# All w_out copies of the weights stored on ScalarE's queue

## The chip, the cores and the metric

The kernel runs on one core of a Trainium2 chip. The metric is the device time of one execution in microseconds (us). PE is TensorE, DVE is VectorE, ACT is ScalarE, POOL is GpSimd and SP is SyncE, which here does nothing but send transfers; ACT sends transfers too, between its own instructions, from one and the same instruction stream.

## The reference, cut to what matters

```python
# q, k, v: 8 x 8 x 576 x 64; a causal window of 64 keys
scores = scale * np.matmul(q, k.transpose(0, 1, 3, 2))
scores = np.where((rel >= 0) & (rel < 64), scores, -1e9)
attn = softmax(scores)
x = (attn @ v).transpose(0, 2, 1, 3).reshape(4608, 512)
h = x @ w_in                       # w_in 512 x 2048, w_out 2048 x 512
g = np.maximum(0.01 * h, h)
out = g @ w_out
```

The weights come as 64-bit floats. The kernel brings them to single precision itself, and splits each single into a high and a low part, so that every product is three products of the parts.

## The kernel before, in words

**The weights.** There are 32 pieces of 128x512 numbers, numbered n: even n is block n/2 of w_in, odd n is block n//2 of w_out. Piece n passes eight small steps, all named with n in a list written by hand (ORDER): `raw` sends the load of the 64-bit words (512 KB, on ACT's queue but for the first three, buffer `raw`, three of them), `bits`, `sign`, `clamp` and `join` on DVE and `abs` on ACT make the single-precision copy `w` (pool tag "o", two buffers), `chi` (function `split`) takes the high part on ACT and also stores `w` to the DRAM tensor `w_single` (256 KB), `rest` takes the low part on DVE. A buffer of `w` is free for a later `join` when the piece in it has had its `rest` and its store has landed. The stored copies are read again much later (`prepare`), to make sums of weight blocks.

**The first stage.** Until about 165 us of the span, PE works through ORDER: attention on pairs of query blocks m (two halves b = 2m, 2m+1: scores `S`, mask and shield `E`, column maximum `P` on POOL, its subtraction `N` or `sub`, `exp`, product with the values `V`, the sums and the quotient `sm`, `rec`, `y` on DVE, transposition `T`, parts of x `H` on ACT and `L` on DVE), and the feed-forward products `M` (h = x w_in) and `W` (g w_out), with `lk`, `gh` on ACT and `gl` on DVE between them. Loads of q, k, v for pair m are sent by SP (`q`, `k`, `v`). In ORDER each engine's instructions stand in the order in which the code issues them, and no engine passes over an instruction that waits.

**The later stages.** A planner (`arrange`) sets the order for the remaining attention and for products that save multiplications (lines 1196 and 1262); all of their inputs come from the first stage.

**Transfer semaphores.** Each transfer that SP or ACT sends takes the next of eight semaphores (DMAHW0 to DMAHW7), over both queues together. Before it is sent, the engine waits until the last transfer that took this semaphore has landed, unless it has already waited for that. In the order below a wait on DMAHW3 is such a wait, or a wait for data.

Of the kernel before, what the change touches and what calls it, by code (L numbers as in the profile page):

```python
# [105 lines left out]
def flat(t):  # L106
    return t.rearrange("p a b -> p (a b)") if len(t.shape) == 3 else t
# [3 lines left out]
def band_attention_ffn(ctx: ExitStack, tc: tile.TileContext, qk, vW, vL, w_in, w_out, eye_mask, out, outT):  # L111
    nc = tc.nc
# [88 lines left out]
    w_single = dram.tile([2, FT, P, 512], F32, name="w_single")  # L201
# [7 lines left out]
    raws, singles = {}, {}  # L209
# [8 lines left out]
    def parts(n):  # L218
        while n // 2 >= len(wi):
            late_weights(len(wi))  # L220
        return (wi, wo)[n % 2][n // 2]
# [27 lines left out]

    def split(n):  # L250
        nc.scalar.copy(flat(parts(n)[0]), singles[n])
        (nc.sync if n % 2 else nc.scalar).dma_start(w_single[n % 2, n // 2], singles[n])

    def rest(n):
        hi, lo = (flat(x) for x in parts(n))
# [200 lines left out]
    def mm2(c, f, part):  # L456


        gh, gl = g.pop((c, f, part.start))
        wh, wl = wo[f]  # L460
        for i in range(part.start // P, part.stop // P):
            split = c == 1 or c == 0 and i < 2
            begin = f == 0 or split and f == half
            end = f == FT - 1 or split and f == half - 1
            if begin:
                pool, tag = (ps_o, f"o{i}")
                if c == 1 and f == 0 and i > 1:
                    pool, tag = ps_e, "st"[i - 2]
                acc[c, i] = pool.tile([P, DM], F32, tag=tag, name=f"acc{c}_{i}_{f}")
            ts = slice(i * P, (i + 1) * P)  # L470
            for n, (a, b) in enumerate(((gh, wh), (gh, wl), (gl, wh))):
                nc.tensor.matmul(
                    acc[c, i], a[:, ts], b, start=begin and n == 0, stop=end and n == 2
                )
            if end:
                due.append(partial(evict, c, i, f, split))

    def evict(c, i, f, split):
        ps = acc.pop((c, i))
        o = probs_of[:, i % 2]  # L480
        nc.scalar.copy(o, ps)
        sums[c, i] = dram.tile([P, DM], F32, name=f"sum{c}_{i}")
        nc.sync.dma_start(sums[c, i], o)
# [26 lines left out]
    def begin(k):  # L510
        steps[k] = mm1(*jobs[k])

    acts = dict(
        S=scores, E=shield, Z=lambda b: add_mask(0, banks[b], False), P=top, N=take, sub=minus, exp=exps, V=values_q, sm=total, rec=inverse, y=product, T=turn, H=high_x, L=low_x,
        raw=fetch_w, bits=bits, sign=sign, abs=size, clamp=clamp, join=join, chi=split, rest=rest, q=load_q, k=load_k, v=load_v,
        X=idle, M=begin, lk=lambda k: steps[k][0](), gh=lambda k: steps[k][1](), gl=lambda k: steps[k][2](), W=lambda k: mm2(*jobs[k]),
        ev=lambda k: due.pop(0)(),
# [188 lines left out]
    for name in late.split():  # L706
        kind = name.rstrip("0123456789")
        n = int(name[len(kind) :])
# [473 lines left out]
    def filled(of, *after):  # L1182
        n = next(fills)
        return n, op("POOL", 0.6, partial(fill, n, of), *tile_free[n % RING], *after, rank=0.2, land=7.0)
# [236 lines left out]
    for s in range(NS):  # L1421
        for f in range(half):
# [4 lines left out]
            for k in range(7):  # L1427
                p, b = 7 * f + k, bank_at(s, BANK[k])
                if p % 4 == 0:
                    made_before = [] if s else [y for x in range(f, min(f + 2, half)) for y in prepared[0, x]]  # L1430
                    n, got = filled(w_first[:, 512 * p : 512 * (p + 4)], *made_before)
# [97 lines left out]
```

## Time and profile before

| what | value |
|---|---|
| median of 3 runs | 859.99 us (859.66, 859.99, 2631.46) |
| the profiled execution | 859.84 us, of which the span is 858.1 us |
| PE busy in the span | 838.6 us (98%) |
| DVE, ACT, POOL busy | 638.9, 376.4, 382.4 us |
| mean granted clock of PE | 0.992 |

The profiled execution is 0.15 us under the median, and 1.7 us of it lie outside the span. A matmul of 128x512 takes 0.39 us by the profile's rows but is followed by the next after 0.23 us, since they overlap; an engine's idle time is what stands in square brackets in a timeline, with what ended it.

### The profile page before, as it was taken

Reading aid. Unit: us, or ns where it says so; the run is one execution under the profiler, and the core shown is the slowest. Engines: PE = TensorE matmul, PEld = TensorE weight load, DVE = VectorE, ACT = ScalarE, POOL = GpSimd, SP = SyncE. Lnnn points to the kernel's source line nnn. Section 1 sums busy time; section 2 is a strip of 40 time slices with the busy share of each in tenths; the row PEclk is TensorE's granted clock in tenths of the full one; section 3 lists DMA queues with packets and bytes.
Section 4 is the critical chain, followed back from the end, with each engine's and each line's share of the span. In section 5 each row is a group of like instructions: output and inputs, shape, how many; then the busy total and the mean of one; then the engine's idle time right before and its main releaser. Section 6 shows DMA issues by size and latency. Waiting matters only on the chain.

```text
span 858.1 us, 16755 instructions
## 1 busy us (share of the span) xinstructions
PE 838.6 (98%) x6736; PEld 682.0 (79%) x6736; DVE 638.9 (74%) x912; ACT 376.4 (44%) x599; POOL 382.4 (45%) x216
## 2 busy tenths in 40 slices
PE   7899999899999999999999999999999999999998
PEld 4777888788788888788788888888888888888886
DVE  5888886576768789798759988676589874546864
ACT  4565654433433435454535443343354433334431
POOL 4322000288788762685876114878863111111110
PEclk9899999999999999999999999999999999999999
DMA  7778578879898979999999898879988997677682
GB/s 270 234 236 268 167 222 297 289 262 327 299 310 308 337 247 296 332 355 375 355 260 316 245 279 268 257 228 298 283 236 240 265 284 202 195 192 192 183 221 96
DMA packets 130861, 225.75 MB, mean 263 GB/s; under 512 B 15840, under 2 KB 53600, under 8 KB 130784
## 3 DMA queue, kind: packets, MB, share of 16 engines
q0 software_dynamic: 53568, 88.09, 37.5%
q10 hardware_dynamic: 34304, 74.16, 26.6%
q1 hardware_dynamic: 42912, 62.43, 21.9%
q8 instruction: 53, 0.87, 0.4%
q14 instruction: 24, 0.20, 0.1%
HBM read 167.28 MB, written 57.26 MB: 262 GB/s over the span
## 4 chain that ended last, share of the span: by engine, by line
PE 51%; DMA 2%; DVE 1%; issue 0%; ACT 0%; ACTq 0%; DVEq 0%
PE z L1262 27%; PE m L1196 22%; PE o L811 2%; DMA p<-w_single 1%; PE s L283 1%; DMA rows<-late_c 1%; DVE pspare L1111 0%; DVE p L1205 0%; DVE pxa L1205 0%; DVE qk L1282 0%; DVE p L1105 0%; ACT p L1108 0%; DVE e L759 0%; DVE late_e L759 0%; DVE s L737 0%
## 5 line engine op out<-in xcount | busy, mean ns | idle before, releaser
L1196 PE MATMUL m<-pfew,p 128*128 128x512 f32 x720 | 170.9, 392 | 0.5 <-DVE pxa L1205 0.5
L1196 PEld LDWEIGHTS m<-pfew,p 128*128 128x128 f32 x720 | 134.1, 188 | 29.2 <-DVE pxa L1205 0.9
L1262 PE MATMUL z<-gs,p 128*128 128x512 f32 (+1 forms) x360 | 86.3, 388 | 0.0
L1000 PE MATMUL acc<-p,gs 128*128 128x512 f32 x324 | 82.3, 399 | 0.0
L1180 POOL DMA_DIRECT2D p<-w_first x42 | 31.7, 754 | 107.8 <-PE m L1196 52.1
L1262 PE MATMUL z<-pspare,p 128*128 128x512 f32 x324 | 78.4, 390 | 0.0
L1262 PEld LDWEIGHTS z<-gs,p 128*128 128x128 f32 x360 | 67.1, 188 | 13.9
L1262 PE MATMUL z<-pxa,p 128*128 128x512 f32 x324 | 78.2, 390 | 0.0
L755 POOL PARTITION_ALL_REDUCE late_o<-late_f x20 | 67.4, 3391 | 13.8 <-ACT late_f L763 8.7
L1208 ACT ACTIVATE p<-p 128x512 f32<-128x512 f32 x60 | 37.8, 631 | 79.4 <-DVE p L1205 79.1
L752 POOL PARTITION_ALL_REDUCE g<-late_f x20 | 36.4, 1856 | 81.3 <-DVE late_f L737 75.2
L1196 PE MATMUL m<-pxb,p 128*128 128x512 f32 x288 | 71.4, 392 | 0.0
L1205 DVE TENSOR_TENSOR p<-m,pxa 128x512 f32<-128x512 f32 x60 | 41.1, 687 | 40.2 <-PE m L1196 39.8
L1262 PEld LDWEIGHTS z<-pxa,p 128*128 128x128 f32 x324 | 60.7, 188 | 12.7
L1000 PEld LDWEIGHTS acc<-p,gs 128*128 128x128 f32 x324 | 60.4, 190 | 13.1
L1262 PEld LDWEIGHTS z<-pspare,p 128*128 128x128 f32 x324 | 60.7, 188 | 12.6
L1205 DVE TENSOR_TENSOR pxa<-m,pxa 128x512 f32<-128x512 f32 x60 | 41.2, 687 | 35.1 <-PE m L1196 34.7
L755 POOL PARTITION_ALL_REDUCE late_o<-e x18 | 58.1, 3259 | 11.5 <-ACT e L763 6.8
L755 POOL PARTITION_ALL_REDUCE late_o<-late_e x18 | 59.1, 3311 | 8.5 <-ACT late_e L763 3.2
L1196 PEld LDWEIGHTS m<-pxb,p 128*128 128x128 f32 x288 | 53.6, 188 | 11.4
L1180 POOL DMA_DIRECT2D p<-w_sums x24 | 18.0, 750 | 87.7 <-PE z L1262 76.9
L991 PE MATMUL h<-pxa,p 128*128 128x512 f32 x228 | 55.6, 391 | 0.0
(201 smaller groups left out, 1625.6 us busy)
## 6 DMA issues: line engine op xcount, KB each, us to landing
p<-w_first POOLq DMA_DIRECT2D x42, 1024.0 KB, 7.1
p<-w_sums POOLq DMA_DIRECT2D x24, 1024.0 KB, 6.2
p<-w_second POOLq DMA_DIRECT2D x18, 1024.0 KB, 6.3
qk<-qk ACTq DMA_DIRECT2D x26, 512.0 KB, 5.9
raw<-w_out ACTq DMA_DIRECT2D x15, 512.0 KB, 4.1
raw<-w_in ACTq DMA_DIRECT2D x14, 512.0 KB, 4.6
more_v<-vL ACTq DMA_DIRECT2D x14, 512.0 KB, 4.6
late_r<-rows SPq DMA_DIRECT2D x54, 128.0 KB, 5.5
```

The lines of the kernel that those rows point to most:

```text
L283: nc.tensor.matmul(ps[j][t, c : c + QB], k[i][s, p], q[s, w, p], start=not begun and (not more or (w, p) == (0, 0)), stop=not begun and no ...
L752: nc.gpsimd.partition_all_reduce(most_of(j), e_of(m)[:, j], P, ReduceOp.max)
L755: nc.gpsimd.partition_all_reduce(sum_of(j), e_of(m)[:, j], P, ReduceOp.add)
L811: nc.tensor.matmul(ps[64 * j : 64 * j + 64, c : c + QB], v[:, 2 * p + j], e_of(m)[:, j, c : c + QB], start=True, stop=True,)
L991: nc.tensor.matmul(ps, a[:, k, :], b[:, k], start=i == 0, stop=i == len(terms) - 1)
L1000: nc.tensor.matmul(acc[c, i], a[:, i * P : (i + 1) * P], b, start=begin and k == 0, stop=n in ends and k == 2)
L1180: nc.gpsimd.dma_start(to, of, max_dma_last_dim=2048)
L1196: nc.tensor.matmul(tiles[b], w[:, 256 * i + 128 * kt : 256 * i + 128 * kt + 128], x_part(OF_X[k], j, kt), start=begin and c == 0, stop=c = ...
L1205: nc.vector.tensor_tensor(to(), tiles[b], x(), ALU.add)
L1208: nc.scalar.activation(to(), to() if b is None else tiles[b], AF.Prelu, alpha=0.01)
L1262: nc.tensor.matmul(tiles[b + i][:, cut], a, x[:, cut], start=begin and f == first and c == 0, stop=f == half - 1 and c == 2, skip_group_ch ...
```

## The change

Stores of `w_single` for odd n were sent by SP, and for even n by ACT. Now ACT sends them all, each right behind the `chi` of its piece.

```diff
     def split(n):
         nc.scalar.copy(flat(parts(n)[0]), singles[n])
-        (nc.sync if n % 2 else nc.scalar).dma_start(w_single[n % 2, n // 2], singles[n])
+        nc.scalar.dma_start(w_single[n % 2, n // 2], singles[n])
```

PE, DVE and POOL keep their rows in the same order; ACT has 16 rows more and SP 16 fewer. Names in the rows: `w1`, `w5` and so on are the copies, `raw2` the words of piece 2, `p15_0` the values of an odd pair, `p14_1` q and k of pair 3 (and 2), `qk0` and `qk1` q and k of the other pairs, `e` the probabilities.

At the start SP stood like this, from the load of `raw2` on, where `w1` is the copy of piece 1:

```order
L216 DMA raw2_278<-w_in 128x1024 [waits DMAHW2_49]
L252 DMA w_single_94<-w1_227 128x512 [waits DMAHW3_49,DVE_49]
L180 DMA p15_0_77<-vW 128x2x520 [waits DMAHW5_49]
L173 DMA p14_1_78<-qk 128x512 [waits DMAHW7_49]
L169 DMA p14_1_78<-qk 128x512 [waits DMAHW1_49]
L180 DMA v_72<-vW 128x2x520 [waits DMAHW2_49,PE_49]
```

and stands like this now:

```order
L216 DMA raw2_278<-w_in 128x1024 [waits DMAHW2_49]
L180 DMA p15_0_77<-vW 128x2x520 [waits DMAHW3_49]
L173 DMA p14_1_78<-qk 128x512 [waits DMAHW4_49]
L169 DMA p14_1_78<-qk 128x512 [waits DMAHW5_49]
L180 DMA v_72<-vW 128x2x520 [waits DMAHW7_49,DMAHW6_49,PE_49]
```

The wait for DVE that stood ahead of the values of pair 1 and of q and k is gone from SP; these loads now wait for semaphores of the first loads alone.

In the middle of the stage SP had four stores in a row, ahead of the loads for pairs 6 and 7:

```order
L173 DMA qk0_83<-qk 128x512 [waits DMAHW5_49,DMAHW2_49,PE_49]
L252 DMA w_single_94<-w5_628 128x512 [waits DMAHW3_49,DVE_49]
L252 DMA w_single_94<-w7_759 128x512 [waits DMAHW5_49,DVE_49]
L252 DMA w_single_94<-w9_861 128x512 [waits DMAHW3_49,DVE_49]
L252 DMA w_single_94<-w11_953 128x512 [waits DMAHW6_49,DVE_49]
L180 DMA v_72<-vW 128x2x520 [waits DMAHW1_49,DMAHW0_49,PE_49]
L169 DMA qk1_84<-qk 128x512 [waits DMAHW4_49,DMAHW1_49]
L180 DMA p15_0_77<-vW 128x2x520 [waits DMAHW2_49,PE_49]
L173 DMA qk1_84<-qk 128x512 [waits DMAHW3_49]
```

and has none now, up to the first partial sums (`sum0`) and the loads for pairs 8 and 9:

```order
L173 DMA qk0_83<-qk 128x512 [waits DMAHW5_49,DMAHW2_49,PE_49]
L180 DMA v_72<-vW 128x2x520 [waits DMAHW6_49,PE_49]
L169 DMA qk1_84<-qk 128x512 [waits DMAHW0_49]
L180 DMA p15_0_77<-vW 128x2x520 [waits DMAHW6_49,DMAHW4_49,PE_49]
L173 DMA qk1_84<-qk 128x512 [waits DMAHW1_49]
L483 DMA sum0_0_1247<-e_76 128x512 [waits DMAHW6_49,DVE_49,Activation_49]
L483 DMA sum0_1_1252<-e_76 128x512 [waits DMAHW1_49,DVE_49,Activation_49]
L173 DMA qk0_83<-qk 128x512 [waits DMAHW2_49,PE_49]
L169 DMA qk0_83<-qk 128x512 [waits DMAHW7_49,DMAHW3_49]
L180 DMA v_72<-vL 128x2x512 [waits DMAHW4_49,PE_49]
L169 DMA qk1_84<-qk 128x512 [waits DMAHW5_49,DMAHW0_49]
L503 DMA w_first_95<-p6_5_87 128x2x256 [waits DMAHW6_49,DVE_49]
```

Eight more stores (pieces 13 to 27) stood between these places; the last five rows and two more like them had the store of piece 27 right ahead of them, and now have `sum0` there.

On ACT, at the pieces 18 to 22, this is what stands now (before, the row of `w19` was not there, and `w18` had no wait):

```order
L216 DMA raw21_1340<-w_out 128x1024 [waits DMAHW7_49,DVE_49]
L251 CAST p9_8_90<-w18_1294 128x512
L252 DMA w_single_94<-w18_1294 128x512 [waits DMAHW2_49]
L441 ACTIVATE g_80<-h1_2_0_1296 128x512 [waits DVE_49,PE_49]
L251 CAST p9_8_90<-w19_1347 128x512 [waits DVE_49]
L252 DMA w_single_94<-w19_1347 128x512 [waits DMAHW3_49]
L216 DMA raw22_1351<-w_in 128x1024 [waits DMAHW4_49]
L446 CAST gs1_82<-g_80 128x512 [waits PE_49,Activation_49]
```

The semaphores 2, 3 and 4 were last taken by SP's loads of pair 8 (`qk0`, `qk0`, `v` in the fence above), so that ACT now waits there for loads of SP to land; those behind it (`raw23`, `w20`, `w21`, `raw25`) wait for the four transfers of SP that follow.

## Rows read from the trace of the kernel before

**Rows 1.** The page: span, and PE's busy time.

```profile
span 858.1 us, 16755 instructions
...
PE 838.6 (98%) x6736; PEld 682.0 (79%) x6736; DVE 638.9 (74%) x912; ACT 376.4 (44%) x599; POOL 382.4 (45%) x216
```

**Rows 2.** What PE waited for, whole span: total us, times, longest us.

```profile
PE o L372 <- DMA p<-vW: 5.6, 1, 5.6
...
PE m L1196 <- DVE pxa L1205: 0.5, 1, 0.5
```

**Rows 3.** Timeline of PE: start us, length us, instruction, [idle before, releaser].

```profile
23.64 2.00 PE L372 MATMUL o<-p,p 128*64 128x65 f32 x32 [5.57 <-DMA p<-vW]
...
31.45 1.69 PE L436 MATMUL h<-pxa,pfew 128*128 128x256 f32 x12
```

**Rows 4.** Timeline of SP's sending, 0 to 140 us.

```profile
6.20 0.33 SPq L216 DMA_DIRECT2D raw<-w_in  x1
15.33 0.33 SPq L252 DMA_DIRECT2D w_single<-w  x1
15.70 1.79 SPq L180 DMA_DIRECT2D p<-vW  x1
...
46.79 23.61 SPq L252 DMA_DIRECT2D w_single<-w  x4
```

**Rows 5.** From sending to landing, the load of values sent at 15.70.

```profile
DMA to landing us min/median/max: 7.8/7.8/7.8
```

**Rows 6.** Timeline of ACT from 15.73 us.

```profile
15.73 1.74 ACTq L216 DMA_DIRECT2D raw<-w_in  x1
17.57 1.09 ACT L329 ACTIVATE e<-s 128x512 f32<-128x512 f32 x2 [1.62 <-PE s L351]
18.55 1.09 ACT L356 ACTIVATE p<-s 128x512 f32<-128x512 f32 x2
```

**Rows 7.** Timeline of DVE at the end of its first long wait.

```profile
24.81 0.16 DVE L379 TENSOR_SCALAR sm<-o 128x4 f32<-128x4 f32 x1 [6.26 <-PE o L372]
```

**Rows 8.** Windows: length, busy us (instructions) by engine, granted clock, DMA share, GB/s.

```profile
14.00:16.00 2.00, 2.00 (x67) 1.43 (x67) 1.93 (x6) 0.75 (x2) 1.50 (x1) 1.00 0.40 141
...
25.00:50.00 25.00, 23.68 (x366) 19.44 (x364) 22.66 (x53) 14.46 (x30) 9.43 (x5) 0.94 0.74 240
50.00:75.00 25.00, 25.00 (x228) 19.77 (x228) 24.25 (x53) 16.55 (x32) 7.57 (x4) 1.00 0.76 230
...
76.00:86.00 10.00, 7.99 (x112) 6.17 (x111) 7.45 (x17) 2.71 (x6) 1.99 (x1) 0.83 0.75 264
150.00:160.00 10.00, 7.52 (x85) 5.89 (x84) 5.37 (x10) 5.74 (x11) 0.00 (x0) 0.83 0.58 213
...
250.00:412.00 162.00, 160.68 (x1522) 130.47 (x1521) 136.69 (x190) 72.30 (x127) 107.09 (x52) 1.00 1.00 322
```

**Rows 9.** Timeline of PE, its next two long waits.

```profile
79.57 0.37 PE L283 MATMUL s<-qk 64*64 64x64 f32 x2 [1.72 <-DMA qk<-qk]
...
153.19 0.33 PE L283 MATMUL s<-qk,qk 64*64 64x64 f32 x2 [2.17 <-ACT e L481]
```

**Rows 10.** Timeline of SP's sending, 136 to 156 us.

```profile
138.36 1.08 SPq L503 DMA_DIRECT2D w_first<-p  x2
...
146.82 7.30 SPq L483 DMA_DIRECT2D sum<-e  x4
```

**Rows 11.** From sending to landing, the two partial sums sent from 146.82.

```profile
DMA to landing us min/median/max: 5.6/5.7/5.8
```

**Rows 12.** From sending to landing, two loads of raw sent from 137.3.

```profile
DMA to landing us min/median/max: 9.1/9.1/9.1
```

**Rows 13.** Timelines of DVE and PE: gl14, and W14, which takes it.

```profile
116.19 0.69 DVE L450 TENSOR_TENSOR gs<-g,gs 128x512 fp32r<-128x512 f32 x1 [0.34 <-ACT gs L446]
...
123.67 2.88 PE L472 MATMUL acc<-pfew,gs 128*128 128x512 f32 x12
```

**Rows 14.** The chi of piece 9 on ACT, and the join of piece 11 on DVE.

```profile
65.24 0.61 ACT L251 CAST pfew<-w 128x512 fp32r<-128x512 f32 x1
...
69.36 0.69 DVE L248 SCALAR_TENSOR_TENSOR w<-raw 128x512 uint32<-128x512 uint32 x1
```

**Rows 15.** From sending to landing, all 32 stores of `w_single`.

```profile
DMA to landing us min/median/max: 2.0/4.2/7.0
```

## The prediction

> **What bounds the kernel now.** I read the page first: PE is busy for 838.6 of 858.1 us [rows 1], so the change can give back only idle time of PE, or time that PE spent at the lower clock, unless it makes new waits. The list of what PE waited for comes next. Its longest entry by far is one wait of 5.6 us for a load of values (`vW`); at the other end stands a wait of 0.5 us on DVE far into the kernel [rows 2]. The timelines then say where these waits lie: all the larger ones are in the first stage, before V of pair 1 at 23.64 us (5.57 us idle) [rows 3], inside the scores of pair 7 at 79.57 (1.72) and before the scores of pair 8 at 153.19 (2.17) [rows 9]. The third reading is SP's own timeline, because the change acts there. SP sends the store of piece 1 at 15.33, nine microseconds after the load before it, and only then the values for which PE waits, at 15.70; from 46.79 to 70.40 it has nothing but four stores to send [rows 4]. The windows show that the transfer engines had room meanwhile: their share is 0.40 from 14 to 16 us [rows 8]. So the first stage is bound, at three places, by when SP gets to send, and it is stores of copies that hold it. Behind the first stage PE hardly waits.
>
> **The change part by part.** All sums are made against the profiled execution's 859.84 us.
>
> *The start, a gain.* The wait for the join of piece 1 leaves SP. The values of pair 1 follow `raw2`, sent at 6.20 [rows 4], with one wait, for the landing of one of the first loads. With the 7.8 us that this load took before [rows 5], or some more for what is ahead of it, it lands at 14.5 to 17, q and k of pair 3 shortly after. Then V of pair 1 waits for its exponentials. These are the two ACT instructions that start at 18.55 and take 1.09 together, so the first is done at 19.1; ahead of them in ACT's stream stand two others from 17.57 and the sending of raw4, which took 1.74 us from 15.73 [rows 6]. The new store of piece 1 adds one sending of 0.33 (SP's at 15.33 took that [rows 4]) ahead of these. If raw4's sending stays at 1.74, V starts at 23.64 - (19.1 + 0.4) = 4.1 us earlier. It overlapped SP's sending of the values, which took 1.79 against 0.33 for others [rows 4]; SP has nothing to send at that time now, so 0.33 is likelier, and then V starts another 1.4 earlier: 5.5. I take 5.0, nearer the second. The 5.57 us idle brought the clock down too (0.94 granted from 25 to 50 [rows 8], that is 3 us of it at half speed), but between V and the first feed-forward product at 31.45 [rows 3] it is DVE that sets the pace: its wait of 6.26 us ended with V's first half at 24.81 [rows 7], and from 25 to 50 it is busy for 22.66 of 25 us [rows 8]. So the first product moves by what V moves, and I count nothing for the clock. **5.0, between 4.1 and 5.5.**
>
> *Pair 7, a gain.* The four stores between 46.79 and 70.40 [rows 4] leave SP; the loads for pairs 6 and 7 then wait only until PE has finished with their buffers, in the worst case the scores of pair 6, long before 79.57. The wait of 1.72 us goes. With it goes a stretch at the lower clock: the granted clock from 76 to 86 is 0.83 [rows 8], which is 10 x 0.17 / 0.5 = 3.4 us at half speed, or 1.7 us of work lost. Together 3.4; the wait alone is the lower end, since DVE, busy for 24.25 of the 25 us before [rows 8], may not hand over its parts so much sooner. **2.8, between 1.7 and 3.4.**
>
> *Pairs 8 and 9 and the stores of w_first, moved.* SP sent these loads and stores in one burst that reaches from 136 to 140 [rows 10], right behind the store of piece 27. Loads of raw sent then took 9.1 us to land [rows 12], and the partial sums from 146.82 took 5.6 to 5.8 [rows 11]. For these sums ACT waits before it can empty the banks that the scores of pair 8 need; that is PE's 2.17 us at 153.19 [rows 9]. Without the stores this burst goes out much earlier, right behind `sum0`, and the sums are sent into a nearly free queue: 2.0 us is the shortest landing of a store of the same size [rows 15], so up to 3.6 us less. PE's wait goes, with the lower clock behind it: 0.83 from 150 to 160 [rows 8], again 1.7 us of work. **3.8, between 2.0 (the burst's raw loads are only partly gone) and 3.9.**
>
> *ACT's holds, a cost.* At pieces 18 to 25 seven of ACT's transfers now wait for SP's burst to land. If that takes the 9.1 us of the crowded loads [rows 12], ACT stands for up to some 5 us at `w18`, with `lk`, `gh` and `chi` queued behind. Who waits for that is PE, through the low part of g: gl14 ends at 116.88 and its product starts at 123.67 [rows 13], a cover of 6.8 us. So I count **0, between -1.5 and 0**; were this cover gone, the 5 us would be PE's. The other 16 sendings on ACT, at 0.33 each, 5.3 us in all over 150 us, stand behind `chi` instructions of 0.61 [rows 14], longer than themselves, and ACT is busy for 16.55 of 25 us where I find it fullest [rows 8]. Nothing for these, since the room that is left covers them; without it they would cost ACT the 5.3 us.
>
> *Later store times.* A store of odd number now leaves behind its `chi`, not behind its `join`. Its buffer must be free for a `join` two pieces on: piece 9 has its `chi` at 65.24 and the join of piece 11 starts at 69.36 [rows 14], 4.1 us later, against a median landing of 4.2 [rows 15]. That is no cost or 0.2 us; with the longest landing it is a rival, below.
>
> The sum: 5.0 + 2.8 + 3.8 = 11.6, and the time 859.84 - 11.6 = 848.2. Its ends are 4.1 + 1.7 + 2.0 - 1.5 = 6.3 (853.5) and 5.5 + 3.4 + 3.9 = 12.8 (847.0); as the clock of the start and a wait or two of 0.3 us are not counted, 845 is the lower end. The rest of the kernel is taken as moved as a whole, since its inputs come from the end of the first stage.
>
> A rule speaks against all of this: by the Trainium skill, "DMA: Bandwidth & Descriptors", section "Issuing engines are not separate DMA queues", transfers of all queues run on the same 16 engines, and the choice of the issuing engine saves only sequencer time, usually small beside the transfer. By it the sum would be about 0. The trace agrees for bandwidth, but the wait of 23.61 us within four stores on SP is time in which the sequencer waits for data, which that rule does not speak of.
>
> **The rivals.**
>
> *No change: it is hidden anyway (859.8).* The choice of the queue moves no bytes. If V of pair 1 were held by something else that ends at 23.6 too, or if the new sendings on ACT pushed the exponentials as far back, the start would give nothing, and without lead the later waits are small: between 858 and 861. It is also what the rule of the Trainium skill above would give. Against it stands that PE's wait at 23.64 ended with the landing itself [rows 3], and the exponentials were done by 19.7 [rows 6].
>
> *The lead is given back in the middle (854).* From 250 to 412 us the transfer engines have a share of 1.00 at 322 GB/s [rows 8], and PE's 0.5 us on `pxa` [rows 2], at the end of this stretch, shows that the other engines are there just in time. If transfers set the pace of that stretch, PE comes 11.6 earlier and waits. Half the lead lost gives 854.0, all of it 859.8. Against it: the stretch begins with the end of the weights, which moves too, and PE is idle for only 1.3 us of its 162 [rows 8].
>
> *Slower: the joins wait for the stores (862).* The place is DVE from 47 to 80 us, where it is nearly always busy [rows 8] and PE follows it. The mechanism is that stores of odd number leave later, and share a queue with the loads of raw. With a landing of 7.0, the longest [rows 15], the join of piece 11 waits 7.0 - 4.1 = 2.9 us, and those of 7 and 9 about 1 each: 5 us. With 9.1 [rows 12], each of the three waits 2 us more and the next two about 1: some 13 us, more than the sum, and 859.84 - 11.6 + 13 = 861.2 or a little more. It decides from landings of about 8.5 us on in this stretch. Against it: the share is 0.76 there [rows 8], and the loads of SP are spread out, no longer in bursts.
>
> **How the numbers follow.** The forecast, 845 to 853.5, gets 0.55; the lead given back, 853.5 to 858, 0.17; no change, 858 to 861, 0.15; slower, above 861, 0.08; below 845 (the counted stretches give more, since the clock stays up in the start as well) 0.05. The predicted time is that of the forecast, 848.2. A range from 844 to 860 leaves out the slower rival, part of the no-change rival and little below, less than 2 in 10. A bound of 2% (17.2 us) is about what a measurement of this kernel can tell from no change; 842.6 and 877.2 are its ends here. Only the outermost part of the last case is under 842.6: faster 0.03, slower 0.02, same 0.95.
>
> **What would show it.** In the profile after, SP sends the values of pair 1 before 9 us, V of pair 1 starts between 18.1 and 19.6, and M0 at 26 to 27.5. The waits inside the scores of pair 7 and before those of pair 8 are gone, and the granted clock there is 1.00. Both feed-forward products that I quote come 7 to 9 us sooner (W14 at about 116), and the first product behind pair 8 some 11. ACT shows a hold of some microseconds at `w18`, without a wait of PE. The forecast is wrong if raw4, which now waits for raw2's landing, stops ACT before the exponentials; if joins in the first 100 us wait for stores by more than 2 us in all; or if PE has new waits behind 160 us, above all at the end of the stretch to 412.

## The result, and the profile after

The changed kernel takes 846.95 us (median of 4 runs, 846.12 to 848.25), beside 859.83 of the kernel before. One execution of the kernel before took 2631 us; the ratio, of the means of the others, leaves it out and is 0.9866, with a 95% interval from 0.9831 to 0.99: 1.3% or 11.5 us less time, clear of no change and inside the 2% that count as the same. The profiled execution took 846.75 us, 13.1 less than the one before.

The page of the profile after answers to [rows 1]:

```profile
span 844.9 us, 16740 instructions
...
PE 833.3 (99%) x6736; PEld 677.0 (80%) x6736; DVE 638.0 (76%) x912; ACT 376.6 (45%) x599; POOL 383.7 (45%) x216
```

PE's busy time fell by 5.3 us though its work is the same: that part of the gain is work that is no longer done at the lower clock. The other part is idle time. The list of what PE waited for (total us, times, longest us) no longer has the values of pair 1 [rows 2] at its head:

```profile
PE s L317 <- DVE pxb L406: 1.5, 2, 0.8
...
PE s L283 <- DMA qk<-qk: 1.1, 2, 0.9
PE m L1196 <- ACT p L1208: 0.9, 1, 0.9
```

SP's timeline of sending answers to [rows 4, 10]:

```profile
6.28 0.33 SPq L216 DMA_DIRECT2D raw<-w_in  x1
6.65 0.57 SPq L180 DMA_DIRECT2D p<-vW  x1
...
47.61 0.55 SPq L180 DMA_DIRECT2D v<-vW  x1
...
91.34 0.72 SPq L173 DMA_DIRECT2D qk<-qk  x1
...
135.52 5.09 SPq L483 DMA_DIRECT2D sum<-e  x4
```

The values of pair 1 leave at 6.65 rather than 15.70, the values of a pair in the middle at 47.61, where four stores stood before and the same load left at 70.51, and the burst for pairs 8 and 9 at 91.34 rather than 136. PE's timeline, at the places of [rows 3, 9]:

```profile
18.23 1.18 PE L372 MATMUL o<-p,p 128*64 128x65 f32 x32 [0.36 <-ACT p L356]
...
24.54 1.70 PE L436 MATMUL h<-pxa,pfew 128*128 128x256 f32 x12
...
57.93 0.73 PE L317 MATMUL s<-away,unit 128*128 128x512 f32 x2 [0.66 <-DVE pxb L406]
...
70.68 0.73 PE L317 MATMUL s<-away,unit 128*128 128x512 f32 x2 [0.81 <-DVE pxb L406]
...
142.44 3.02 PE L1000 MATMUL acc<-p,gs 128*128 128x512 f32 x12
```

V of pair 1 has moved from 23.64 to 18.23 and its 32 products take 1.18 rather than 2.00 us. M0 moved from 31.45 to 24.54, which is more. The scores of pairs 7 and 8, at 79.57 and 153.19 before, no longer wait for `qk` or for ACT's `e`; instead two small waits for DVE (`pxb`) stand in front of the shields of pairs 6 and 7.

PE's rows are the same in both kernels, so the start of each can be subtracted from that of the same row before. I call the difference the **lead**; it shows where time was won and where it went again:

| place (start before) | lead after | what changed it |
|---|---|---|
| V of pair 1 (23.64) | 5.4 | the wait of 5.57 is now 0.36 |
| M0 (31.45) | 6.9 | V and what follows at full clock |
| 49.27 | 7.3 | |
| 76.82, shield of pair 7 | 6.1 | waits for `pxb`: 0.8 and 0.5 lost |
| 123.67, W14 | 9.6 | pair 7's wait gone, clock up |
| 159.30, behind pair 8 | 14.0 | waits of 2.2 and 0.3 gone, clock up |
| 222.95 | 14.3 | |
| 427.20 and the end | 13.2 | 1.1 lost in one wait, for ACT |

The windows say the same of the clock (columns as in [rows 8]); the first two are the stretches around pairs 7 and 8, the last the middle:

```profile
66.00:76.00 10.00, 9.19 (x128) 6.98 (x126) 9.81 (x19) 5.11 (x10) 4.74 (x2) 1.00 0.65 219
136.00:146.00 10.00, 10.00 (x104) 8.11 (x104) 6.55 (x13) 5.74 (x11) 0.00 (x0) 1.00 0.70 249
240.00:402.00 162.00, 160.32 (x1521) 130.16 (x1516) 136.92 (x192) 74.11 (x129) 106.81 (x51) 1.00 1.00 325
```

The granted clock is 1.00 where [rows 8] had 0.83. In the middle PE is idle for 1.68 of 162 us, 0.36 more than before: the lead is not given back there in this execution.

### The profile page after: what moved, and what is told of

It reads as the page before. It is cut to its first block, busy times and chain, and to the rows that moved or that the text cites. A ratio compares the mean times of both kernels' runs of the same rounds, so it can differ in the third digit from the quotient of the medians.

```text
span 844.9 us, 16740 instructions
## 1 busy us (share of the span) xinstructions
PE 833.3 (99%) x6736; PEld 677.0 (80%) x6736; DVE 638.0 (76%) x912; ACT 376.6 (45%) x599; POOL 383.7 (45%) x216
## 4 chain that ended last, share of the span: by engine, by line
PE 84%; DMA 9%; DVE 3%; ACT 1%; issue 1%; ACTq 0%; POOL 0%; SPq 0%; DVEq 0%
PE z L1262 27%; PE m L1196 24%; PE acc L1000 9%; PE h L991 9%; PE h L436 4%; PE acc L472 4%; PE s L283 4%; PE o L811 3%; DMA w_sums<-p 2%; DMA v<-vL 2%; DMA qk<-qk 2%; DMA w_single<-w 1%; DMA raw<-w_out 1%; DMA w_first<-pfew 1%; DMA raw<-w_in 1%
```

## The experiments

Two theories stood against each other at first. **Order on SP:** a store that waits for its data holds the loads behind it on SP; the gain is the sum of three such places (pieces 1, 5 to 11, and 27). **ACT's queue, or fewer sendings on SP:** the place of the stores in the stream doesn't matter, only which engine sends them and how many; the expectations call this one "queue mix". Later two smaller questions came up: what the clock gave in the start, and what the later stores cost. Medians of the kernel before beside these runs were 858.7 to 859.0; executions of one kernel spread by 3 to 9 us, so where 2 us matter the leads say where time went, and only for the execution that was profiled.

**u1_sp: the change, but the store of piece 1 back on SP.**

```diff
-        nc.scalar.dma_start(w_single[n % 2, n // 2], singles[n])
+        (nc.sync if n == 1 else nc.scalar).dma_start(w_single[n % 2, n // 2], singles[n])
```

> The changed kernel, but the store of piece 1 alone goes back to SP. Theory 'order on SP' (the gain is loads that no longer stand behind a store on SP): the values of pair 1 are sent at about 15.5 us again, V of pair 1 starts at 23.6, the lead of 6.9 us that the changed kernel has at the first feed-forward product is gone, the other two places keep theirs: about 853.8 us. Theory 'queue mix' (the gain comes from 16 stores sharing ACT's queue, a little from each): one store of 16, about 847.8 us.

Measured: 853.0 us (851.09 to 856.28, 7 runs), ratio 0.9939 [0.9912, 0.9967]. Two pieces of its trace, SP's sending and PE's wait:

```profile
15.26 0.33 SPq L252 DMA_DIRECT2D w_single<-w  x1
15.64 0.57 SPq L180 DMA_DIRECT2D p<-vW  x1
```

```profile
22.93 2.00 PE L372 MATMUL o<-p,p 128*64 128x65 f32 x32 [4.93 <-DMA p<-vW]
```

One store brings the wait of the start back, almost whole, and V's products at 2.00 us with it. The lead is 0.7 at V of pair 1; the gains of pairs 7 and 8 stay (3.3 and 4.4 us of lead). So the start is worth 6 to 7 us, about half of the gain, and it hangs on one store.

**o1_act: the kernel before, with the store of piece 1 alone on ACT.**

```diff
-        (nc.sync if n % 2 else nc.scalar).dma_start(...)
+        (nc.sync if n % 2 and n != 1 else nc.scalar).dma_start(...)
```

> The kernel before, with the store of piece 1 alone on ACT. Theory 'order on SP': V of pair 1 at 18.2 us and the first feed-forward product 6.9 us sooner; the two later waits as in the kernel before: about 853 us. Theory 'queue mix': one of 16, about 859 us.

Measured: 852.17 us (851.19 to 854.23, 6 runs), ratio 0.9924 [0.9895, 0.9953]. V of pair 1 starts at 18.48, the lead is 6.5 at 28 us and 6.5 at the end. The two runs add up: by the ratios 0.61% and 0.76% make 1.37%, against 1.34% of the whole change. The scores of pair 7 wait 1.66 us for `qk` as before; but the wait of pair 8, which was expected to stay at 2.17, is smaller, though no store but that of piece 1 has moved:

```profile
146.89 0.32 PE L283 MATMUL s<-qk,qk 64*64 64x64 f32 x2 [1.00 <-ACT e L481]
```

The clock stays at 1.00 behind it, and the lead grows there by 2.7 us.

**spl_sp: the kernel before; the store of piece 1 stays on SP, but is sent behind the values of pair 1 and q and k of pair 3.** No store goes to ACT that didn't before.

```diff
+        if m == 3:            # in the load of q, which stands behind that of k
+            nc.sync.dma_start(w_single[1, 0], held_single.pop())
...
-        (nc.sync if n % 2 else nc.scalar).dma_start(...)
+        if n == 1:
+            held_single.append(singles[n])
+        else:
+            (nc.sync if n % 2 else nc.scalar).dma_start(...)
```

> The kernel before, all stores on the queues that they had, but the store of piece 1 is issued on SP three loads later, behind the values of pair 1 and q and k of pair 3. Nothing moves to ACT. Theory 'order on SP': as with that store on ACT, V of pair 1 near 18 us and about 853 us. Theory 'queue mix': no stores on ACT more than before, 859.8 us.

Measured: 854.45 us (850.89 to 859.63, 10 runs), ratio 0.9959 [0.9936, 0.9983]. SP's sending, and PE (line numbers are some higher in this kernel; L171 is the store):

```profile
6.71 0.56 SPq L182 DMA_DIRECT2D p<-vW  x1
...
15.19 0.33 SPq L171 DMA_DIRECT2D w_single<-w  x1
15.63 0.55 SPq L182 DMA_DIRECT2D v<-vW  x1
```

```profile
17.86 1.15 PE L379 MATMUL o<-p,p 128*64 128x65 f32 x32
...
22.70 0.69 PE L379 MATMUL o<-v,e 128*64 128x65 f32 x16 [1.93 <-DMA v<-vW]
```

With the values ahead of it the same store on the same engine lets V start at 17.86, a lead of 5.8. What is late next is again the load right behind the store: the values of pair 2, sent at 15.63 (13.71 in the changed kernel), for which PE now waits 1.93. The lead falls from 7.7 to 5.7 with that wait and is 5.0 at pair 7; in the medians 4.5 us of time are won. (The profile is of the fastest of the ten executions, 850.89, and has a lead of 8.9 at its end.) Neither ACT's queue nor the number of sendings differs here; the order alone does it. That ACT's queue is the better place, by the 2.3 us between this run and the last, is likely by the wait of 1.93 but not shown in time: the intervals overlap.

**odd_pool: the kernel before, with the stores of odd number on POOL's queue rather than ACT's.**

```diff
-        (nc.sync if n % 2 else nc.scalar).dma_start(...)
+        (nc.gpsimd if n % 2 else nc.scalar).dma_start(...)
```

> The kernel before, with the 16 stores of odd number on POOL's queue: SP is as free as in the changed kernel, ACT sends none more than before. Theory 'order on SP': all three waits of PE go as in the changed kernel, 845 to 849 us, if no column maximum on POOL is held for long behind a store that waits for its join; such holds would add their own length. Theory 'queue mix' (stores on ACT's queue make the gain): no gain, 859 us or more.

Measured: 848.6 us (845.51 to 852.12, 4 runs), ratio 0.9891 [0.9848, 0.9933]. POOL's queue gives most of the gain as well. A store holds what stands behind it there too; on PE:

```profile
16.85 1.13 PE L351 MATMUL s<-p,p 128*128 128x512 f32 x2 [1.39 <-POOL p L337]
```

POOL waits for DVE, whose join of piece 1 ends at 13.75, and sends at 14.08, with a column maximum behind it. V of pair 1 starts at 20.11: 1.9 later than with the store on ACT.

**u11_sp and u27_sp: the change, but one store back on SP, of piece 11 or of piece 27.**

```diff
-        nc.scalar.dma_start(...)
+        (nc.sync if n == 11 else nc.scalar).dma_start(...)     # u27_sp: n == 27
```

> The changed kernel, but the store of piece 11 alone goes back to SP, ahead of the loads for pairs 6 and 7. Theory 'order on SP': SP stands until the join of piece 11 at about 63.6 us, the last load for pair 7 is sent at about 65.5 and lands some 7 us later, PE waits about 1.5 us inside the scores of pair 7 and may lose clock behind it: 848.5 to 850 us. Theory 'queue mix': about 847.8 us.

Measured: 849.4 us (847.59 to 853.71, 4 runs), ratio 0.989 [0.9849, 0.9931]. Its SP, and its PE at the scores of pair 7:

```profile
62.65 0.33 SPq L252 DMA_DIRECT2D w_single<-w  x1
63.07 0.55 SPq L180 DMA_DIRECT2D v<-vW  x1
```

```profile
72.27 0.27 PE L283 MATMUL s<-qk 64*64 64x64 f32 x2 [1.69 <-DMA qk<-qk]
```

The wait of pair 7 is back at its old size, with the store of one piece ahead of the loads. The lead at W14 is 7.2 rather than 9.6: 2.4 us less, between the two ends that the prediction gave this term. The time is 2.4 us over the changed kernel's too, but there the intervals overlap.

> The changed kernel, but the store of piece 27 alone goes back to SP. Theory 'order on SP': the burst of loads and stores for pairs 8 and 9 goes out behind that store again, the partial sums land late, PE waits before the scores of pair 8 and loses clock: the 4.4 us of lead gained there are lost, about 851.3 us. Theory 'queue mix': about 847.8 us.

Measured: 850.0 us (847.41 to 852.22, 4 runs), ratio 0.9889 [0.9852, 0.9926]. The burst for pairs 8 and 9 stands behind that store until 126; PE at the scores of pair 8:

```profile
142.08 0.33 PE L283 MATMUL s<-qk,qk 64*64 64x64 f32 x2 [0.85 <-ACT e L481]
```

Here the expectation was too simple: 0.85 of the 2.17 us came back, the clock stays at 1.00, and the lead behind pair 8 is 12.8 rather than 14.0. The burst leaves 9 us ahead of the sums (before it was 7 to 10 us), yet PE loses less. The sums take 6.0 us to land, as before, but PE's other work fills 5.9 us of that rather than 4.2. So the late burst costs 1.2 to 1.4 us in this profile; the 3.0 us of the medians can't be told from it, as the intervals overlap.

**before_x22: the kernel before, with 22 idle products (128x512) on PE in the wait for the values of pair 1.** Nothing moves on SP; only PE's clock can change.

```diff
-... exp3 T0 v1 V2 V3 ...
+... exp3 T0 v1 X22 V2 V3 ...
```

> The kernel before, with 22 idle matmuls between T of pair 0 and V of pair 1, some 5.0 us that lie within PE's wait of 5.57 us; they add no work behind it. Theory 'clock' (the wait cost PE's clock too, and 1.5 of the 6.9 us of lead at the first feed-forward product are the clock's): granted clock 1.00 from 20 to 28 us, the first product 1.5 us sooner, about 858.3 us. Theory 'DVE sets the pace there' (as in the prediction): the first product at 31.4 again, 859.8 us.

Measured: 857.92 us (856.45 to 862.7, 10 runs), ratio 0.9998 [0.9976, 1.0019]: no measurable gain. Its timeline of PE, and windows of the kernel before and of this one (granted clock third from the end):

```profile
17.90 5.26 PE L508 MATMUL idle<-p 128*128 128x512 f32 x22
23.25 1.15 PE L372 MATMUL o<-p,p 128*64 128x65 f32 x32
...
29.18 1.70 PE L436 MATMUL h<-pxa,pfew 128*128 128x256 f32 x12
```

```profile
22.00:24.00 2.00, 0.36 (x7) 0.39 (x9) 0.00 (x0) 0.00 (x0) 0.00 (x0) 0.50 1.02 388
24.00:26.00 2.00, 2.00 (x32) 1.88 (x30) 1.17 (x5) 0.40 (x1) 0.26 (x1) 0.50 0.43 167
26.00:28.00 2.00, 2.00 (x50) 1.35 (x53) 2.00 (x5) 0.23 (x1) 1.52 (x1) 0.51 0.45 111
```

```profile
24.00:26.00 2.00, 2.00 (x80) 1.57 (x75) 2.00 (x8) 0.63 (x1) 1.10 (x1) 1.00 0.62 199
26.00:28.00 2.00, 2.00 (x36) 1.62 (x26) 2.00 (x6) 1.13 (x3) 0.97 (x2) 1.00 0.90 320
```

In the kernel before, the clock stands at 0.50, the lower level, from 22 us, in the idle time, to 28. With PE kept busy it stays at 1.00, and from V to M0 it takes 29.18 - 23.25 = 5.9 us rather than 7.8. So in these 8 us PE at half clock set the pace and not DVE, whose rows come earlier as well. The lead of 2.3 at M0 shrinks to 1.4 at 43 us and to 0.8 from 80 to 150. The 2.2 at the end of this one profile come from another place, pair 8, where nothing was changed:

```profile
150.83 0.32 PE L283 MATMUL s<-qk,qk 64*64 64x64 f32 x2 [0.62 <-ACT e L481]
```

The wait is 0.62 rather than 2.17, the clock stays at 1.00, and the lead grows by 3.1. So that the clock moves M0 is shown; it is worth nothing that the timed runs can tell, with a bound of about 2 us.

**h57: the change, but the stores of pieces 5 and 7 stay on SP**, run twice.

```diff
-        nc.scalar.dma_start(...)
+        (nc.sync if n in (5, 7) else nc.scalar).dma_start(...)
```

> The changed kernel, with the stores of pieces 5 and 7 back on SP, where they leave right behind their joins and hold no load that is needed soon. Theory 'later stores cost the joins': the join of piece 9 no longer waits 1.3 us for the store of piece 7, PE's waits of 0.66 and 0.81 us before the scores of pairs 6 and 7 shrink, and the time falls by up to 1.3 us, about 846 us. Rival: those two waits come from DVE's own load and stay, 847 us.

Measured: 846.6 us (844.94 to 847.78, 4 runs), ratio 0.9865 [0.9834, 0.9895]. In the changed kernel the store of piece 7 leaves ACT at 49.57, takes 6.9 us to land, and DVE's join of piece 9 waits for it:

```profile
56.58 0.69 DVE L248 SCALAR_TENSOR_TENSOR w<-raw 128x512 uint32<-128x512 uint32 x1 [1.31 <-DMA w_single<-w]
57.19 0.68 DVE L406 TENSOR_TENSOR pxb<-t,pxb 128x512 fp32r<-128x512 f32 x1
```

Behind that join stands the `pxb` for which PE waits 0.66 at 57.93. In h57 the join runs without a wait:

```profile
55.25 0.68 DVE L248 SCALAR_TENSOR_TENSOR w<-raw 128x512 uint32<-128x512 uint32 x1
```

and the lead is 0.8 better there, as far as 14.9 at the end against 13.2. To see whether that is time, both kernels ran once more, on one chip:

> The changed kernel once more, beside the kernel with the stores of pieces 5 and 7 left on SP, on one chip. Both theories expect what it gave before: 847, between 845.5 and 849, with a ratio of 0.986.

> As the change, but the stores of pieces 5 and 7 stay on SP. Theory 'later stores cost a join': the join of piece 9 waits 1.3 us for the store of piece 7 in the changed kernel, PE loses 0.8 at pair 6 for it, and the profile of this kernel without that wait had 1.7 us less of span; then it is 1 to 2 us faster than the changed kernel on the same chip, 845 to 846. Rival 'given back behind': the time is that of the changed kernel within 0.5 us, since the products behind 400 us wait for the parts of x that much longer.

Measured: the changed kernel 847.21 us (845.3 to 849.83, 5 runs), ratio 0.9866 [0.9842, 0.989]; h57 846.27 us (843.64 to 847.4, 5 runs), ratio 0.9848 [0.9822, 0.9874]. The difference of 0.9 has the expected sign but the intervals overlap; whether h57 is faster stays open. The profile of h57_r5 has the 0.8 again, and loses 1.1 where PE waits for ACT's `late_n`, at 209 us. That wait is 0.5 to 2.1 us long in all these profiles, 1.0 in the kernel before, 0.7 in one profile of the changed kernel and 1.9 in the other, so nothing ties it to a store.

**all_sp: the kernel before, with the stores of even number on SP as well**, the opposite of the change.

```diff
-        (nc.sync if n % 2 else nc.scalar).dma_start(...)
+        nc.sync.dma_start(...)
```

> The kernel before with the other 16 stores (even pieces) moved to SP as well, so that SP sends all 32. Theory 'order on SP': a store costs by the load that stands behind it, and every load that PE waits for stands behind a store of odd number already, which leaves later than the even one beside it; the values of pair 1 still leave at 15.7, and V of pair 1 starts at 23 to 24.5. Only raw2 leaves some 7 us later (behind the store of piece 0, at 13.4 rather than 6.2), at a time when DVE waits anyway. So 858 to 863. Rival 'each store on SP costs the same': 16 fewer gave 13 us, 16 more take as much, 870 to 874.

Measured: 862.26 us (859.84 to 865.07, 8 runs), ratio 1.0037 [1.0018, 1.0056]. Sixteen stores fewer on SP gave 11.5 to 13 us; sixteen more cost 3.6. The number of sendings is not what counts. Its SP and PE show two places that do:

```profile
13.77 0.43 SPq L216 DMA_DIRECT2D raw<-w_in  x1
...
29.56 10.23 SPq L252 DMA_DIRECT2D w_single<-w  x3
...
41.39 0.62 SPq L173 DMA_DIRECT2D qk<-qk  x1
42.06 0.47 SPq L169 DMA_DIRECT2D qk<-qk  x1
```

```profile
20.49 0.66 PE L398 MATMUL t<-unit,y 128*128 128x128 f32 x4 [2.93 <-DVE y L391]
...
48.17 0.27 PE L283 MATMUL s<-qk,qk 64*64 64x64 f32 x2 [1.91 <-DMA qk<-qk]
```

`raw2` now stands behind the store of piece 0 and leaves at 13.77 rather than 6.20. DVE waits for it, with the quotients of the first pairs behind it; I had taken DVE to wait then anyway. V of pair 1 still starts at 24.43, 0.8 late, since its values hold it. The larger part of the 3.6 is lost later: the loads of q and k behind the three stores from 29.56 leave at 41.39 and 42.06 (36.97 and 37.63 before), and PE waits 1.91 for them at 48.17. The lead falls there from -0.5 to -2.5. That only `raw2` would leave later was wrong, though the time lies in the range expected.

## Why the prediction was right

The mechanism and the sum hold: 11.6 forecast, 13.1 measured in the profiles and 11.5 in the ratio, 847 against 848.2. Point by point, by the prediction's own steps:

*The start, 5.0 (4.1 to 5.5): mis-sized.* The values left at 6.65 and landed 9.3 us later (7.8 was taken), by 16.0; V then waited for its exponentials alone, started at 18.23, and so far the step was right, 5.4. It had raw4's sending fall from 1.74 to 0.33 because SP would have nothing to send at that time. It fell to 0.50, but the reason isn't borne out: in u1_sp SP sends the values within 0.03 us of it, and it takes 0.45. The size came out by luck there. Last, "I count nothing for the clock" failed: M0 has a lead of 6.9, as PE's products between V and M0 run at full clock. before_x22 shows this step alone: 1.9 us from V to M0 with no load moved. DVE's 22.66 of 25 us misled me. That is a mean over a window in which PE at half clock came first and DVE later, and the window begins at 25, while the clock stood at 0.50 from 22 us on. How much of these 1.5 us is left at the end isn't shown: in before_x22 most of its lead at M0 is gone by 80 us.

*Pair 7, 2.8 (1.7 to 3.4): right in size, of two parts.* The wait of 1.72 went, and u11_sp brought it back with one store. From 49 us to W14 the lead grew by 9.6 - 7.3 = 2.3 net, after 1.3 lost in the two waits for `pxb`; the gain itself is 3.6, a little over the upper end. In all six profiles with the store of piece 11 on SP, PE waits 1.66 to 1.93 us there for `qk`; in the seven without, it doesn't.

*Pairs 8 and 9, 3.8 (2.0 to 3.9): right in cause; 4.4 in these two profiles, less in others.* The sums sent from 135.52 landed in 3.4 to 3.6 us rather than 5.6 to 5.8 [rows 11], PE's two waits for ACT's `e` of 2.2 and 0.3 are gone, and the clock gave the other 1.9. The cause is borne out by every profile here: in the six with the burst behind the store of piece 27 (before, before_x22, o1_act, spl_sp, all_sp, u27_sp) the first two sums take 5.0 to 6.2 us to land and PE waits 0.6 to 2.4 at the scores of pair 8; in the seven with the burst ahead of it they take 3.2 to 3.9 and PE doesn't wait. The size is not steady: the clock fell behind the waits of 2.17 and 2.42 (before and all_sp) and stayed at 1.00 behind the four of 0.62 to 1.51. Measured against those four profiles the early burst is worth 1.3 to 2.2 us, not 4.4. So part of the 13.1 is the execution of the kernel before that was profiled, and the forecast was made from that same execution.

*ACT's holds, 0 (-1.5 to 0): right, for another reason.* A hold of up to 5 us at `w18` was expected. ACT's timeline in the changed kernel:

```profile
97.43 0.33 ACTq L252 DMA_DIRECT2D w_single<-w  x1
...
98.63 0.33 ACTq L252 DMA_DIRECT2D w_single<-w  x1
...
100.30 0.34 ACTq L216 DMA_DIRECT2D raw<-w_in  x1
100.74 0.62 ACT L446 CAST gs<-g 128x512 fp32r<-128x512 f32 x1 [1.49 <-PE acc L472]
```

SP's loads landed in 6.0 to 6.8 us and not in the 9.1 of [rows 12]: the one that `w18` waits for at 97.41, so that it leaves at 97.43, before its `chi` is done at 97.54, and `w19` leaves with its `chi`. Only `raw22` is held, about 1.3 us, until the load of values sent at 93.44 has landed at 100.3; the `gh` behind it waits for PE beyond that. The cover of 6.8 us was not needed.

*Later store times, 0 to 0.2: too low.* The join of piece 9 waits 1.31, for a store that took 6.9 us to land. h57 puts the cost at 0.8 us of lead on PE; in the timed runs it isn't shown. DVE's waits for stores were 2.3 us in all before and are 2.7 after, so few of them are new; this one has PE behind it.

What was to show it came, but for ACT's hold, and at these places sooner than forecast: M0 at 24.54 rather than 26 to 27.5, W14 at 114.05 rather than 116, the row behind pair 8 14.0 us earlier rather than 11. Of the signs of being wrong one showed, in small: joins in the first 100 us wait for stores for 1.8 us in all (2 was the mark), raw4 doesn't stop ACT, and PE has a new wait of 0.9 us at 413 us. One end of the 2% range was mis-added: 859.84 and 17.2 make 877.0.

The rivals: *no change* is ruled out by the interval. The sentence of the Trainium skill behind it ("DMA: Bandwidth & Descriptors", section "Issuing engines are not separate DMA queues"), that another issuing engine saves only sequencer time, would have made the sum about 0; 11.5 to 13 us were measured. The time in which a sequencer stands at a transfer that waits for its data, nine microseconds at the start here, is what it doesn't speak of, and spl_sp won 4.5 us without another engine. *Given back in the middle* did not happen in this profile (0.36 of 162 us); 1.1 us of lead went in one wait for ACT at 413 us, which the second profile of the same kernel doesn't have. But it isn't ruled out for every execution: the profiles of u11_sp and odd_pool lose 5.5 and 4.1 us of lead behind 160 us, in waits for `late_n`, `qk` and ACT's `p`. Both are of executions slower than their medians. *Slower through the joins* is real as a mechanism, with 1.3 us on DVE rather than 13.

## What to carry to other kernels

In these traces a transfer that waits for its data held every transfer behind it on its engine, on SP for up to 23.6 us within four stores, on POOL at the start and on ACT at raw22; so look in the sending engine's timeline for the store that leaves just before a late load, and move that one store: behind the load, or to an engine with nothing urgent behind it. One store (piece 1) held half the gain here, and 16 more stores on the same queue cost only 3.6 us, so count what stands behind a store and not the stores. A wait that drops PE's clock costs more than its length: at pair 8, waits of 2.5 us went with 4.4 us of lead. And a profile is of one execution: the same wait at pair 8 measured 0.6 to 2.4 us in six profiles.

## What the runs showed of the hardware

The length of a sending varies, and no run shows why. In the kernel before, SP's sending of the values and ACT's of raw4 start within 0.03 us and take 1.79 and 1.74 us [rows 4, 6]. With SP silent, the same sending of raw4 takes 0.50 in the changed kernel:

```profile
15.99 0.50 ACTq L216 DMA_DIRECT2D raw<-w_in  x1
...
17.57 1.09 ACT L356 ACTIVATE p<-s 128x512 f32<-128x512 f32 x2
```

That looks like the price of two engines sending at once, but in u1_sp the two start within 0.03 us of each other as well, and SP's takes 0.57 (15.64, shown above) and ACT's 0.45:

```profile
15.67 0.45 ACTq L216 DMA_DIRECT2D raw<-w_in  x1
```

One execution of the changed kernel (after_r5) has a gap on PE in the start that nothing in the trace explains. With it the lead at M0 is 5.1 rather than 6.9, so it is of the size of the effects sought here; a single profile isn't enough to tell 2 us:

```profile
23.04 0.27 PE L283 MATMUL s<-p 64*64 64x64 f32 x1 [1.64 <-issue]
```
